# Pooled attention into a tanh-shrink MLP: batch 2's queries load behind batch 1's turns, batch 1's values go through GpSimd, the last queries load at a phase's end

## The chip, the cores and the metric

The kernel runs on one core of a Trainium2 chip. The metric is the device time of one execution in microseconds (us), the median of several runs. Engines are named as in the profile: PE is TensorE, PEld its weight loads, DVE is VectorE, ACT is ScalarE, POOL is GpSimd, and SP is SyncE, whose queue issues most of the DMAs.

## The reference

Eight batches, eight heads, 576 positions, head size 64. Keys and values are averaged over groups of 8 positions, which leaves 72 of them; attention runs over these, and its output goes through a two-layer network without biases, whose activation is h - tanh(h).

```python
k_p = k.reshape(B, H, Sp, pool, D).mean(axis=3)      # Sp = 576 / 8 = 72
v_p = v.reshape(B, H, Sp, pool, D).mean(axis=3)
scores = scale * np.matmul(q, k_p.transpose(0, 1, 3, 2))
scores = scores - np.max(scores, axis=-1, keepdims=True)
attn = np.exp(scores)
attn = attn / (np.sum(attn, axis=-1, keepdims=True) + 1e-09)
attn_out = np.matmul(attn, v_p)
x = attn_out.transpose(0, 2, 1, 3).reshape(B * S, H * D)   # 4608 x 512
h = x @ w_in                                               # 512 x 2048
out = (h - np.tanh(h)) @ w_out                             # 2048 x 512
```

## The kernel before

**Groups.** The 4608 rows are worked as nine groups of 512: group g below 8 is the first 512 positions of batch g, and group 8 collects the last 64 positions of all eight batches (the "tails", two batches to a tail block). A group has an h phase (16 blocks of four matmuls with `w1b`, `h_mms`, tanh on ACT and the subtraction on DVE in `h_act`) and an o phase (16 units of four matmuls with `w2b`, `o_mms`, whose banks are copied by `o_store` and stored from a list `stores`). While PE works on group g, the attention of batch g + 1 runs in between.

**Attention of a batch** is cut into four query blocks (five units where a tail block belongs to it: groups 1, 2, 4 and 6 carry tails 0, 1, 2 and 3). Each unit goes through the steps

- "s": scores on PE (`s_mms`), row maximum and subtraction on DVE (`s_shift`);
- "e": the exponential on ACT (`s_exp`) into the tile E;
- "t": the turn of E into ET by a DMA transpose that SP issues (`e_turn_dma`), for two units at once in the main loop;
- "a": weights times values on PE (`av_mms`, reads ET and VB), then reciprocal and multiply on DVE (`normalise`) into x_sb;
- "x": the turn of x_sb into xT, the h phase's operand, again a DMA transpose on SP (`x_turn_dma`).

**Order.** The schedule is written by hand: each engine runs its instructions in program order, and the framework only adds semaphores. In the main loop (line 697 on) a table `plan` says after which h block (negative keys, block i has key i - 16) or o unit (keys from 0) a step is issued. Group 0's o phase has a loop of its own (`for u in range(16)`, line 657), with batch 1's attention unit by unit: `s_unit` (each unit turned by itself) and `a_unit`. PSUM has eight banks; the scores of phase 0 use the pairs `PA = (0, 1)` and `PB = (2, 3)`, its output blocks banks 4 to 7.

**Loads.** `load_for(g)` issues on SP the values of batch g + 1, the queries and keys of batch g + 2, and for odd g the tail queries of that pair of batches. Values and keys are pooled by GpSimd (`pool_v`, `pool_k`) and placed in VB and, after a turn by DMA (`k_turn_dma`), in KB (`k_place_kT`). Queries are cast to bf16 by ACT (`q_cast`) and turned by DMA (`q_turn_dma`). Tail queries are loaded (`tail_pieces`), cast by GpSimd (`tail_cast`) and turned (`turn_tail`). For batch 1 some of this is done by PE: `q_turn_pe`, `k_turn_pe`, and `v_pool_pe`, which pools the values into a PSUM bank.

SP's order in group 0's o phase is thus: keys and queries of batch 2; the four turns of E; tail 0's queries; two x turns; the turns of batch 2's queries, of its keys and of tail 0; `load_for(1)`, with tail 1's queries last; four output stores; and then, in group 1, the first turn of batch 2.

## Time and profile before

| | |
|---|---|
| runs shown | 313.4, 314.0 and 1074.03 us; median 314.0 us |
| the profiled execution | 312.61 us, its span 310.9 us |
| granted TensorE clock, mean | 0.989 |
| busy: PE, DVE, ACT, POOL | 290.0, 181.0, 140.7, 109.4 us |
| group 1 starts its h phase | 61.09 us |
| group 2 | 95.34 us |

Times in the profile count from the span's start. In a row of the timeline the first number is the start, the second the time that the row covers, then come engine, line, operation, the tile written and the tile read, and in brackets how long the engine stood idle before it and what ended that. The list of waits gives who waited for whom, the total in us, how many times, and the longest. In the DMA rows the last number is the median time from issue to landing. Matmuls are pipelined, so the time from one start to the next is what a matmul costs PE.

### The profile page before, as it was taken

Reading aid. Unit: us, or ns where it says so; the run is one execution under the profiler, and the core shown is the slowest. Engines: PE = TensorE matmul, PEld = TensorE weight load, DVE = VectorE, ACT = ScalarE, POOL = GpSimd, SP = SyncE. Lnnn points to the kernel's source line nnn. Section 1 sums busy time; section 2 is a strip of 40 time slices with the busy share of each in tenths; the row PEclk is TensorE's granted clock in tenths of the full one; section 3 lists DMA queues with packets and bytes.
Section 4 is the critical chain, followed back from the end, with each engine's and each line's share of the span. In section 5 each row is a group of like instructions: output and inputs, shape, how many; then the busy total and the mean of one; then the engine's idle time right before and its main releaser. Section 6 shows DMA issues by size and latency. Waiting matters only on the chain.

```text
span 310.9 us, 4511 instructions
## 1 busy us (share of the span) xinstructions
PE 290.0 (93%) x1724; PEld 149.7 (48%) x1747; DVE 181.0 (58%) x251; ACT 140.7 (45%) x183; POOL 109.4 (35%) x97
## 2 busy tenths in 40 slices
PE   4779997999699998999999999999999999999995
PEld 1447954444354454445544554454445544444443
DVE  4596767469733993298419942984199427304700
ACT  1467744158323762267236632672364335315511
POOL 6545715019810592079108810791080000000000
PEclk9599999999999999999999999999999999999999
DMA  7999999989987978898999698978802640020023
GB/s 231 219 231 298 216 285 166 153 241 326 222 188 230 319 122 151 242 327 117 215 255 303 111 187 209 334 146 180 257 14 44 164 120 0 0 103 34 0 62 74
DMA packets 88981, 55.15 MB, mean 177 GB/s; under 512 B 62752, under 2 KB 76448, under 8 KB 88960
## 3 DMA queue, kind: packets, MB, share of 16 engines
q1 hardware_dynamic: 81648, 46.48, 61.2%
q0 software_dynamic: 6032, 7.60, 12.6%
q10 hardware_dynamic: 1280, 0.79, 0.8%
q8 instruction: 13, 0.21, 0.3%
q14 instruction: 8, 0.07, 0.1%
HBM read 36.70 MB, written 9.44 MB: 148 GB/s over the span
## 4 chain that ended last, share of the span: by engine, by line
PE 73%; DMA 14%; DVE 4%; ACT 3%; SPq 2%; issue 2%; ACTq 0%; DVEq 0%
PE PS L428 31%; PE PS L385 31%; DMA ET<-E 7%; DMA k_raw<-in_k_dram 5%; PE PS L338 4%; PE PS L274 2%; PE PS L407 2%; DMA xT<-x_sb 1%; PE PS L255 1%; DVE x_sb L360 1%; ACT E L302 1%; DMA ETl<-El 1%; DMA out_dram<-o_sb 1%; DVE sh L289 1%; DVE mx L286 1%
## 5 line engine op out<-in xcount | busy, mean ns | idle before, releaser
L428 PE MATMUL PS<-w2b,gT 128*128 128x512 bf16 (+2 forms) x570 | 131.7, 373 | 1.0
L399 DVE TENSOR_TENSOR gT<-PS,t_sb 128x1024 bf16<-128x1024 f32 x64 | 77.2, 1220 | 63.1 <-ACT t_sb L398 63.1
L385 PE MATMUL PS<-xT,w1b 128*128 128x512 bf16 x448 | 100.8, 379 | 0.3 <-DMA xT<-x_sb 0.2
L398 ACT ACTIVATE t_sb<-PS 128x1024 f32<-128x1024 f32 x64 | 65.6, 1025 | 43.3 <-PE PS L385 43.3
L428 PEld LDWEIGHTS <-gT 128*128 128x128 bf16 x592 | 54.3, 98 | 58.0 <-issue 0.8
L385 PEld LDWEIGHTS <-w1b 128*128 128x128 bf16 x512 | 49.3, 98 | 56.9 <-DMA xT<-x_sb 0.7
L449 ACT COPY o_sb<-PS 128x512 f32<-128x512 f32 x33 | 19.4, 587 | 83.9 <-PE PS L428 82.7
L207 POOL TENSOR_TENSOR v_raw<-v_raw 128x1280 f32<-128x1280 f32 x6 | 17.4, 2906 | 67.0 <-DMA v_raw<-in_v_dram 62.3
L302 ACT ACTIVATE E<-sh 128x576 bf16<-128x576 f32 x32 | 21.8, 683 | 21.4 <-DVE sh L289 21.4
L286 DVE TENSOR_REDUCE mx<-PS 128x8 f32<-128x576 f32 x36 | 27.0, 749 | 3.3 <-PE PS L274 3.3
L289 DVE TENSOR_TENSOR sh<-PS,mx 128x576 f32<-128x576 f32 x36 | 27.3, 758 | 1.2
L359 DVE RECIPROCAL rden<-PS 128x8 f32<-128x8 f32 x36 | 7.4, 206 | 32.4 <-PE PS L338 32.4
L192 POOL TENSOR_TENSOR k_raw<-k_raw 128x1280 f32<-128x1280 f32 x7 | 20.3, 2905 | 8.1 <-DMA k_raw<-in_k_dram 8.0
L360 DVE TENSOR_TENSOR x_sb<-PS,rden 128x512 bf16<-128x512 f32 x32 | 22.1, 691 | 1.1
L338 PE MATMUL PS<-VB,ET 128*128 128x130 bf16 (+2 forms) x192 | 16.7, 222 | 5.2 <-DMA ET<-E 4.8
L338 PEld LDWEIGHTS <-ET 128*128 128x128 bf16 x192 | 13.2, 98 | 13.0 <-DMA ET<-E 6.8
L243 ACT CAST q_bf<-q_raw 128x1024 bf16<-128x1024 f32 x14 | 14.5, 1040 | 5.9 <-DMA q_raw<-in_q_dram 5.9
L407 PE MATMUL PS<-xT,w1b 128*128 128x256 bf16 x128 | 15.3, 273 | 0.7 <-ACT xT L377 0.7
L229 POOL COPY KB<-kT 64x288 bf16<-64x288 bf16 x12 | 5.1, 424 | 26.3 <-DMA kT<-kd 26.0
L274 PEld LDWEIGHTS <-qT 128*128 128x128 bf16 x128 | 10.2, 100 | 7.9 <-ACT qT L520 0.8
L385 PE MATMUL PS<-xTt,w1b 128*128 128x512 bf16 x64 | 14.0, 379 | 0.0
L420 DVE TENSOR_TENSOR gT<-PS,t_sb 128x512 bf16<-128x512 f32 x16 | 10.9, 691 | 5.0 <-ACT t_sb L419 3.4
(72 smaller groups left out, 167.6 us busy)
## 6 DMA issues: line engine op xcount, KB each, us to landing
out_dram<-o_sb SPq DMA_DIRECT2D x32, 256.0 KB, 2.6
k_raw<-in_k_dram SPq DMA_DIRECT2D x14, 512.0 KB, 8.1
q_raw<-in_q_dram SPq DMA_DIRECT2D x13, 512.0 KB, 7.1
v_raw<-in_v_dram SPq DMA_DIRECT2D x12, 512.0 KB, 4.7
w1b<-in_moe_w_in_dram POOLq DMA_DIRECT2D x4, 512.0 KB, 8.9
w2b<-in_moe_w_out_dram POOLq DMA_DIRECT2D x4, 512.0 KB, 19.8
v_raw<-in_v_dram POOLq DMA_DIRECT2D x2, 512.0 KB, 13.8
k_raw<-in_k_dram POOLq DMA_DIRECT2D x1, 1024.0 KB, 13.4
```

Source lines behind the costliest of these rows:

```text
L192: eng.tensor_tensor(out=r[:, :, 0:4, :], in0=r[:, :, 0:4, :], in1=r[:, :, 4:8, :], op=ALU.add)
L286: nc.vector.reduce_max(out=mx.rearrange("p k h o -> p k (h o)"), in_=sc, axis=AX.X)
L289: nc.vector.tensor_tensor(out=sh[:, :, :, :], in0=sc, in1=mx.to_broadcast([128, 2, 4, G]), op=ALU.subtract)
L302: nc.scalar.activation(out=E[:, e, :, :].rearrange("p t c -> p (t c)")[:, 0:NK], in_=sh.rearrange("p k h c -> p (k h c)"), func=ACT.Exp, s ...
L338: nc.tensor.matmul(PS[ps, banks[half], D1 * h : D1 * (h + s1 - s0)], lhsT=ET[:, t, c0 : c0 + (ps.stop - ps.start)], rhs=VB[kb][:, t, s0:s1 ...
L360: nc.vector.tensor_tensor(out=x_sb, in0=ps[:, :, :, 0:D], in1=rden.to_broadcast([128, 2, 4, D]), op=ALU.mult,)
L385: nc.tensor.matmul(PS[:, bank, :].rearrange("p (j c) -> p j c", j=R), lhsT=w1b[:, fb, i * 128 : (i + 1) * 128], rhs=xT_of(g)[:, :, fb, :], ...
L398: nc.scalar.activation(out=t_sb[:, :, :], in_=ps, func=ACT.Tanh)
L399: nc.vector.tensor_sub(out=gT[:, i : i + 2, :], in0=ps, in1=t_sb[:, :, :])
L407: h_mm_last[0] = nc.tensor.matmul(PS[:, bank, 256 * s : 256 * s + 256].rearrange("p (j c) -> p j c", j=2), lhsT=w1b[:, fb, (2 * n + s) * 1 ...
L428: nc.tensor.matmul(PS[:, bank, 0 : c1 - c0], lhsT=gT[:, i, tb * 128 : (tb + 1) * 128], rhs=w2b[:, i, c0:c1], start=(i == 0), stop=(i == NH ...
L449: eng(out=o_sb[:, :], in_=PS[:, bank, :])
```

## The change

1. In the lead-in, the turned keys of batch 1 go to banks 6 and 7 instead of 0 and 1.
2. In group 0's o phase, batch 2's queries are no longer loaded ahead of it; SP issues them behind the fourth turn of E. Their cast, and the turns of batch 2's keys and queries (keys first now), are issued behind the second x turn.
3. Batch 1's values are pooled by PE right behind the first scores, in bank 7; ACT copies them to a new tile v_sm in SBUF, and GpSimd multiplies them into VB, where DVE did it from PSUM behind unit 3. GpSimd's pooling of batch 2's keys stands behind that.
4. The score units of phase 0 follow units 0, 1, 2 and 4 (before: 0, 1, 3 and 5), its values units 7, 8, 9 and 10 (before: 6, 7, 9 and 10).
5. Tail 0's queries are loaded behind the query turn and ahead of `load_for(1)`; their turn is issued behind it and ahead of the four stores.
6. Tails 1 to 3: `load_for` no longer loads them. They are loaded behind o unit 11 of groups 1, 3 and 5 and cast by GpSimd behind it (before: cast after o unit 0, turned at o unit 11), and turned in the h phase of the next group, behind the first turn of E.
7. The plan: the third values unit moves behind o unit 9, to the fourth. With a tail, the tail's exponential and turn move from o unit 5 to 4, and the third and fourth values units from 9 and 10 to 9. In group 1 the steps between the first exponential and the third scores are 2 to 3 h blocks later, the first two values units stand behind o units 6 and 7 (before: 4 and 5), and the last two behind 10.

```diff
+    v_sm = const.tile([128, NT, 1, D], FP32, name="v_sm")
...
-    kps = flat(0, NT * 128)
+    kps = flat(6, NT * 128)
     k_turn_pe(1, 0, NT, kps)
...
-            if g % 2:
-                r += tail_pieces((g + 2) // 2)
         run(r)
...
     after(load_rows(k_rows, k_raw[0], 2, 0, 2), held)
-    run(k_pieces(2)[1:] + q_pieces(2))
-    pool_k(2, nc.gpsimd)
+    run(k_pieces(2)[1:])
...
     def s_unit(n, bk):
         s_mms(s_block(1, n), bk)
         sh = s_shift(bk)
+        if n == 0:
+            nc.scalar.copy(
+                out=v_sm.rearrange("p t o d -> p (t o d)"),
+                in_=v_pool_pe(1, 7).rearrange("p t o d -> p (t o d)"),
+            )
+            v_place(1, v_sm, nc.gpsimd)
+            pool_k(2, nc.gpsimd)
         s_exp(sh, slot(4 + n))
         e_turn_dma(slot(4 + n), n % 2, n % 2 + 1)
...
-        if u == 3:
-            v_place(1, v_pool_pe(1, 0), nc.vector)
-            s_unit(2, PB)
-        if u == 5:
-            s_unit(3, PA)
+        if u == 2:
+            s_unit(2, PA)
+        if u == 4:
+            s_unit(3, PB)
+            run(q_pieces(2))
+        if u == 7:
+            a_unit(0, PA)
+        if u == 8:
+            a_unit(1, PB)
+            x_turn_dma(x1[0], 1, 0, 2)
+        if u == 9:
+            a_unit(2, PA)
+        if u == 10:
+            a_unit(3, PB)
+            x_turn_dma(x1[1], 1, 2, 2)
+            q_cast(2, se, 0, 2)
+            q_cast(2, se, 2, 4)
+            k_turn_dma(2)
+            k_place_kT(2, ge)
+            q_turn_dma(2)
             run(tail_pieces(0))
             tail_cast(0)
-        if u == 6:
-            a_unit(0, PB)
-            q_cast(2, se, 0, 2)
-            q_cast(2, se, 2, 4)
-        if u == 7:
-            a_unit(1, PA)
-            x_turn_dma(x1[0], 1, 0, 2)
-        if u == 9:
-            a_unit(2, PB)
-        if u == 10:
-            a_unit(3, PA)
-            x_turn_dma(x1[1], 1, 2, 2)
-            q_turn_dma(2)
-            k_turn_dma(2)
-            k_place_kT(2, ge)
-            turn_tail(0)
             load_for(1)
...
+    turn_tail(0)
     run(stores)
...
-                8: [("a", 2)],
-                9: [("a", 3), ("x", 1)],
+                9: [("a", 2), ("a", 3), ("x", 1)],
             }
             if g == 1:
-                plan[-10], plan[-7] = plan.pop(-12), plan.pop(-9) + plan.pop(-8)
+                plan[-10], plan[-7], plan[-5] = plan.pop(-12), plan.pop(-9), plan.pop(-8)
+                plan[-2], plan[-1] = [("e", 1), ("t", 0)], plan.pop(-3)
             if tail is not None:
                 units.append((s_tail(tail), av_tail(tail), slot_tl))
                 plan[3].append(("s", 4))
-                plan[5] += [("e", 4), ("t", 2)]
-                plan[10] = plan.pop(9)
-                plan[9] = plan.pop(8)
+                plan[4] += [("e", 4), ("t", 2)]
+                if g == 1:
+                    plan[6], plan[7] = plan[4][:1], plan.pop(5)
+                    plan[4] = plan[4][1:]
+                    plan[10] = plan.pop(9)
                 plan[12] = [("a", 4), ("x", 2)]
...
                 e_turn_dma(units[2 * n][2], 0, 2 if n < 2 else 1)
+                if tail and n == 0:
+                    turn_tail(tail)
...
                 pool_k(nb + 1, nc.gpsimd)
-                if nb % 2 == 0:
-                    tail_cast(nb // 2)
...
                 if u == 11 and nb % 2 == 0:
-                    turn_tail(nb // 2)
+                    run(tail_pieces(nb // 2))
+                    tail_cast(nb // 2)
```

## The prediction

> **What bounds the kernel now.** I read the page first, then what TensorE (PE) waits for, then its timeline, then the SP queue and the landing times of its DMAs. The page's first block, and two rows of PE's waits (us in all, times, longest):
>
> ```profile
> PE 290.0 (93%) x1724; PEld 149.7 (48%) x1747; DVE 181.0 (58%) x251; ACT 140.7 (45%) x183; POOL 109.4 (35%) x97
> ...
> PE PS L338 <- DMA ET<-E: 4.8, 4, 2.4
> ...
> PE PS L255 <- ACT qT L520: 0.7, 1, 0.7
> ```
>
> PE is busy for 93% of the span. Where the waits stand, in PE's timeline (start, us, matmuls; in brackets the idle time before them):
>
> ```profile
> 42.42 0.41 PE L274 MATMUL PS<-KB,qT 128*128 128x144 bf16 x4
> ...
> 45.51 1.25 PE L525 MATMUL PS<-v_raw,ident 128*128 128x320 bf16 x8
> ...
> 51.35 0.53 PE L338 MATMUL PS<-VB,ET 128*128 128x130 bf16 x6 [1.71 <-DMA ET<-E]
> ...
> 56.18 0.35 PEld L338 LDWEIGHTS <-ET 128*128 128x128 bf16 x6 [0.63 <-DMA ET<-E]
> ...
> 61.09 6.20 PE L385 MATMUL PS<-xT,w1b 128*128 128x512 bf16 x28
> ...
> 83.65 0.53 PE L338 MATMUL PS<-VB,ET 128*128 128x130 bf16 x6 [2.44 <-DMA ET<-E]
> ...
> 95.34 4.48 PE L385 MATMUL PS<-xT,w1b 128*128 128x512 bf16 x20
> ...
> 124.81 0.72 PE L338 MATMUL PS<-VB,ETl 128*64 128x130 bf16 x12 [1.36 <-DMA ETl<-El]
> ...
> 189.92 4.49 PE L385 MATMUL PS<-xT,w1b 128*128 128x512 bf16 x20 [0.24 <-DMA xT<-x_sb]
> ...
> 213.71 0.53 PE L338 MATMUL PS<-VB,ET 128*128 128x130 bf16 x6 [0.54 <-DMA ET<-E]
> ```
>
> and two rows of the chain of waits (start, us, instructions):
>
> ```profile
> 53.10 1.73 PE PS L428 x8
> ...
> 99.82 0.25 PE PS L274 x4
> ```
>
> All but the 0.7 us are waits for a DMA turn (transpose). The list names four for ET, 4.8 us in all; 1.71, 2.44 and 0.54 stand here, so the fourth is about 0.1. With 0.63 (the weight load of phase 0's fourth values unit), 1.36, 0.24 and 0.7 they add up to 7.7 us. No matmul is added or removed, and what else PE idles lies in the start and the last store, which the diff leaves alone: a gain can hardly exceed 7.7 us, 2.5%.
>
> **Phase 0 (output blocks of group 0, attention of batch 1; 41.4 to 61.09).** Its turns share the DMA engines with batch 2's query load, and SP issues everything in order:
>
> ```profile
> 45.64 7.18 SPq L311 DMA_TRANSPOSE ET<-E  x4
> 52.87 2.27 SPq L154 DMA_DIRECT2D tl_raw<-in_q_dram  x2
> ...
> 59.04 2.13 SPq L249 DMA_TRANSPOSE qT<-q_bf  x1
> ```
>
> The landing times of the DMAs issued between 34 and 64 (count, KB each, median us from issue):
>
> ```profile
> q_raw<-in_q_dram SPq DMA_DIRECT2D x2, 512.0 KB, 13.7
> tl_raw<-in_q_dram SPq DMA_DIRECT2D x2, 128.0 KB, 4.1
> ...
> ET<-E SPq DMA_TRANSPOSE x4, 4.7
> ...
> xT<-x_sb SPq DMA_TRANSPOSE x2, 3.3
> ...
> qT<-q_bf SPq DMA_TRANSPOSE x1, 4.5
> ```
>
> And ACT's casts of the queries:
>
> ```profile
> 51.50 1.98 ACT L243 CAST q_bf<-q_raw 128x1024 bf16<-128x1024 f32 x2
> ```
>
> The queries took 13.7 us, and ACT could cast them at 51.50; the first turn, issued at 45.64, ended in PE's row at 51.35, 5.7 us later. With the queries behind the fourth turn, I give the turns the median 4.7 us or less: the first lands by 50.3. In the new order PE reaches it after eight output blocks of four matmuls, four score units and the pooling of the values. By the chain's rows a block is 0.865 us (1.73 for eight matmuls) and a score unit 0.25; the pooling is 1.25. The first block stands ahead of the first score at 42.42, so it is there at 42.42 + 1.25 + 7 x 0.865 + 4 x 0.25 = 50.7. So 1.71 and 0.63 go, and the phase would end 2.3 us sooner, near 58.8. The keys' turn in other PSUM banks takes away the 0.7 us wait for ACT, but the score behind it still needs the copied keys, whose copies wait for the last subtraction on VectorE; I price that edit at nothing. Without that it would gain 0.7.
>
> The values of batch 1 get one ACT copy, which ends before ACT's first exponential could start, and a GpSimd multiply instead of VectorE's:
>
> ```profile
> 75.79 1.80 POOL L219 TENSOR_TENSOR VB<-v_raw,mask 128x960 bf16<-128x960 f32 x1
> 57.77 0.61 POOL L162 CAST tl_bf<-tl_raw 128x512 bf16<-128x512 f32 x1 [6.45 <-DMA tl_raw<-in_q_dram]
> ```
>
> 1.80 us from about 44.4 ends at 46.2, four before its reader. Batch 2's key pooling, behind it on GpSimd, comes about a microsecond later, and SP turns the keys only after the last x turn. Cost: nothing; if the values were later than 50.7, one for one.
>
> **What becomes late.** SP's four turns took 7.18 us from 45.64, to 52.8; with the pooling no longer between the second and third score, and one exponential after the other as before, I let them end at 52.2, and the queries go out then. Nearest rows for their landing: 6.0 us behind the values (below, batch 3's) and 13.7 above. I take 6.0, since by then no weights are left in flight: 58.2 (ends: 56 and 66). x's second turn goes out three blocks, four values units (0.53 at most) and about 1 us of normalising after 50.7, near 56, with 3.3 us to land, behind the queries, so I start the next h phase at 59.5 and not at 58.8. ACT's two casts (1.98) end at 60.3, SP's turn of the queries goes out then and lands 4.5 us later, as it did before, at 64.8. The first scores of the h phase stand behind seven h groups: 59.5 + 7 x 0.865 = 65.5. Hidden by 0.7 us. ACT's output copies queue behind the casts and are needed by the fifth h group at 63; hidden too.
>
> In a sentence that the sum does not need: the Trainium skill, DMA: Bandwidth & Descriptors, sections Specifications and Anatomy of one DMA, gives about 358 GB/s from HBM and 2 us fixed, so an estimate of 5 us for 1 MB, and the queries would land at 57.2; the sum would be the same within its bounds, as the wait below decides.
>
> **Group 1 (61.09 to 95.34).** SP's queue there:
>
> ```profile
> 62.88 1.22 SPq L165 DMA_TRANSPOSE tl_T<-tl_bf  x1
> 64.19 1.04 SPq L114 DMA_DIRECT2D v_raw<-in_v_dram  x2
> ...
> 68.83 1.69 SPq L154 DMA_DIRECT2D tl_raw<-in_q_dram  x2
> 70.62 4.09 SPq L452 DMA_DIRECT2D out_dram<-o_sb  x4
> 75.84 1.99 SPq L311 DMA_TRANSPOSE ET<-E  x1
> ...
> 83.31 1.36 SPq L311 DMA_TRANSPOSE ET<-E  x1
> ```
>
> and the landing times of what was issued between 64 and 76:
>
> ```profile
> q_raw<-in_q_dram SPq DMA_DIRECT2D x2, 512.0 KB, 6.0
> tl_raw<-in_q_dram SPq DMA_DIRECT2D x2, 128.0 KB, 8.4
> ...
> ET<-E SPq DMA_TRANSPOSE x1, 7.8
> ```
>
> The first turn of batch 2 is issued at 75.84 and lands 7.8 us later, at 83.6: it is drained behind the loads and four stores. In the new order the queries' turn (60.3 to 62.5) is followed by the tail queries (2.27 us of issue), so the value loads leave at 64.8, 0.6 later than before. Tail 1's two loads (1.69 us) no longer stand between the keys and the stores, tail 0's turn (1.22) does. The tail lands at 64.8 + 4.1 = 68.9 at the latest, GpSimd's cast adds 0.61, and SP comes to the turn at about 69.4, so hardly a wait. Net: +0.6 - 1.69 + 1.22, so the turn lands at 83.7; between 82 (only the lost tail counts) and 85.5 (the queries 2 us later). The scores of the second unit are now two h groups later, and their exponential stands behind a query cast, ready near 75.0, just ahead of 75.8.
>
> PE comes to the first values unit after output block 6 instead of 4, at 59.5 + 13.8 + 1.4 (five score units) + 6.05 = 80.8, and waits about 2.9 us to 83.7. So phase 0's gain is not additive: the wait swallows it. What counts is how much remains behind the landing: 95.34 - 83.65 = 11.69 us before, two output blocks fewer now, 9.96. Group 2 starts at 93.7: **-1.6 us**. The second pair's turn went out at 83.31 behind the first, and I leave it there: with 3.3 us like the x turns it lands near 87, ahead of its readers after block 10 (83.7 + 4 x 0.865 + two values units = 88). The x turn behind them goes out near 90 and lands by 93.5.
>
> **Groups 2 to 6.** The tail's exponential and turn go ahead of the output copy and of the first x turn, one block earlier, and ACT is free there: 1.36 goes. The third values unit moves one block (0.865) later, more than 0.1 and 0.54: both go. In the tail groups the last x turn is a block earlier, more than 0.24: goes. Together 1.36 + 0.1 + 0.54 + 0.24 = **-2.2 us**, or nothing of it if the tail's turn or a value comes as much later as it is moved. The tail's loads move ahead of the value loads (1.7 to 2.3 us of SP) in groups 1, 3 and 5, and its turn (1.22) ahead of a query turn; the values they delay have slack:
>
> ```profile
> 109.83 1.80 POOL L219 TENSOR_TENSOR VB<-v_raw,mask 128x960 bf16<-128x960 f32 x1
> ...
> 114.96 0.52 PE L338 MATMUL PS<-VB,ET 128*128 128x130 bf16 x6
> ```
>
> 111.6 to 114.96 is 3.3 us, the smallest cover of that edit; beyond it a late value costs one for one. The sum is -1.6 - 2.2 = -3.8 us. The profiled execution took 312.61 (span 310.9), so 308.8 on its scale; the median of the runs shown is 314.0, the lowest 313.4, their middle 313.7, and from there I predict 309.9.
>
> **Rivals.**
> *A. The queries come late.* A landing at 62 instead of 58.2 moves the value loads and all behind them by 3.8: group 2 starts at 97.5, +2.2, total 0.0: 313.7. For it: they took 13.7 once. Against: the w2b loads of that time are gone.
>
> *B. Slower: SP stands at tail 0's turn.* That turn now waits for a load, for GpSimd's cast, and has four stores and batch 2's first turn behind it in SP's order. It decides once the tail lands after about 76: then its turn (1.22), four stores and the E turn cannot go out before 80 and all of the gain is spent. With the 13.7 us that the queries once took, from 64: landing 77.7, cast 78.3, tail turn 79.5, half of the 4.09 that four stores took, so the E turn out at 81.6 and landed at 89.4. That is 5.7 later than forecast: -3.8 + 5.7 = +1.9, 315.6. Against it: 4.1 and 8.4 us are the tail's own rows.
>
> *C. The clock.* PE's longer wait at the first values unit may cost its clock. Start of the kernel and the old wait (window, length, busy time and count of each engine, granted clock, DMA share, GB/s):
>
> ```profile
> 8.00:10.00 2.00, 0.10 (x2) 0.11 (x3) 1.17 (x4) 0.83 (x1) 0.10 (x1) 0.50 1.20 252
> ...
> 12.00:14.00 2.00, 2.00 (x15) 1.10 (x13) 0.30 (x1) 1.47 (x3) 2.00 (x4) 0.50 1.24 205
> ...
> 82.00:84.00 2.00, 0.35 (x6) 0.35 (x7) 0.36 (x1) 0.00 (x0) 1.92 (x3) 1.00 1.11 250
> ```
>
> After idle gaps near the start the clock was 0.50 for the 4 us of work from 10 to 14; the 2.44 us wait left it at 1.00. If 2.9 us is past the edge, 4 us at half clock cost 2.0: 311.9. The Trainium skill, TensorE: Matmul & The Clock Gate, Part 1, puts the edge at an idle window of about 3.4 us and the recovery at as much busy time; by it 2.9 us is just safe, and this trace does not show the edge itself.
>
> *D. Everything goes.* If the first turn lands by 80.8, group 2 starts at 90.8, -4.5, with -2.2: 307.0. Against it: 1 MB of stores still stands ahead.
>
> **Numbers.** Forecast 0.55, A 0.17, B 0.07, C 0.12, D 0.09. A difference of 2%, about 6.3 us, is what a measurement tells from none: D alone (and luck in the forecast) is faster by that, 0.10; B must grow to twice its price, or A join it, to be slower by that, 0.05; within it 0.85. The range, 306.8 to 314.4, holds D's end, the forecast with turn landings of 82 to 85.5, C and most of A.
>
> **What would show it.** Right: no wait at the first and fourth values unit of phase 0, h of group 1 starting near 59.5, no wait for qT in it, the first values unit of group 1 at 83 to 84.5 after a wait of 2 to 3.5 us, group 2 at about 93.7, and no waits for ETl, ET or xT from there. Wrong: a PE wait for qT or xT near 60 to 66, SP idle ahead of tail 0's turn, a granted clock under 1 near 84, or GpSimd's values late in groups 2, 4 or 6.

## The result, and the profile after

| | before | changed |
|---|---|---|
| first chip: median (runs) | 314.16 us (313.4 to 314.32) | 310.0 us (309.31 to 310.66), ratio 0.9875 [0.9843, 0.9908] |
| second chip: median (runs) | 311.83 us (311.16 to 314.01) | 309.67 us (308.75 to 310.83), ratio 0.9927 [0.9901, 0.9953] |
| profiled execution (its span) | 312.61 (310.9) us | 310.13 (308.4) us, a second one 309.71 (308.0) us |

The comparison leaves out the run of 1074.03 us, which stands by itself; the median of 314.16 still counts it, without it it is 314.0. The changed kernel is faster by 0.5% to 1.6%, inside the 2% that the forecast called "no change", and its median is 0.1 us from the forecast. The profiled executions say less: 2.5 us between them, where 3.8 had been worked out.

The page's first block of the changed kernel, and a row of what PE waits for:

```profile
PE 292.1 (95%) x1747; PEld 150.4 (49%) x1747; DVE 179.5 (58%) x250; ACT 140.9 (46%) x184; POOL 111.2 (36%) x98
...
PE PS L339 <- DMA ET<-E: 2.7, 1, 2.7
```

Of the four waits for ET, 4.8 us, one is left, and it is longer than any before; the waits for ETl and for xT are no longer in the list. Two small ones have come, at the first score (the keys) and at the start of the h phase. PE's timeline, at the places shown of before (line numbers are one higher now):

```profile
42.59 0.41 PE L275 MATMUL PS<-KB,qT 128*128 128x144 bf16 x4 [0.88 <-ACT KB L230]
...
50.72 0.52 PE L339 MATMUL PS<-VB,ET 128*128 128x130 bf16 x6
...
54.44 0.53 PE L339 MATMUL PS<-VB,ET 128*128 128x130 bf16 x6
...
60.12 6.21 PE L386 MATMUL PS<-xT,w1b 128*128 128x512 bf16 x28 [0.84 <-DVE o_sb L450]
...
84.71 0.53 PE L339 MATMUL PS<-VB,ET 128*128 128x130 bf16 x6 [2.74 <-DMA ET<-E]
...
94.67 4.48 PE L386 MATMUL PS<-xT,w1b 128*128 128x512 bf16 x20
...
122.71 0.72 PE L339 MATMUL PS<-VB,ETl 128*64 128x130 bf16 x12
...
187.41 4.49 PE L386 MATMUL PS<-xT,w1b 128*128 128x512 bf16 x20
```

Phase 0's first values unit (50.72) and the fourth (54.44) start without a wait. The h phase of group 1 starts 0.97 us earlier than before, but its first values unit 1.06 us later. From that unit to the next group it is 94.67 - 84.71 = 9.96 us, where it was 11.69. Behind it no bracket stands any more, neither at the tail's values (122.71) nor at group 4's h phase (187.41).

When group 7 (its full operand, xT) and group 8 (the collected tails, xTt) start, from the rows of the h phase's line, first before, then changed (ns min/median/max, first and last start):

```profile
L385 PE MATMUL PS<-xT,w1b x4: 379/379/379, 251.8 to 252.4; 128*128 128x512 bf16 x4
...
L385 PE MATMUL PS<-xTt,w1b x3: 379/379/379, 279.4 to 279.8; 128*128 128x512 bf16 x3
```

```profile
L386 PE MATMUL PS<-xT,w1b x3: 378/380/380, 248.8 to 249.2; 128*128 128x512 bf16 x3
...
L386 PE MATMUL PS<-xTt,w1b x3: 378/379/380, 276.4 to 276.8; 128*128 128x512 bf16 x3
```

So the 2.5 us come about as follows. The first score stands 0.2 later (42.59 for 42.42). From there to group 2 it is 52.08 us instead of 52.92: -0.8. Groups 2 to 6, from group 2's start to group 7's, take 154.1 instead of 156.4: -2.3. Group 7 is the same, and from group 8's start to the end it is 32.0 instead of 31.5: +0.5. The second profiled execution of the changed kernel gives 51.92, 154.0 and 32.0. The last piece, which the diff doesn't touch, is 31.4 to 32.1 in all the executions profiled here, of whichever kernel. The -0.8 rests on one execution of the kernel before: with its group 0 and group 1 unchanged, the same stretch takes 52.33 us in experiment 4 and, less the 1.66 us of a fallen clock, 52.05 in experiment 3. So what phase 0 and group 1 gain is 0 to 1 us, within the scatter; only the -2.3 is clear of it.

What makes the first values unit of group 1 late stands in the SP queue:

```profile
45.80 6.01 SPq L312 DMA_TRANSPOSE ET<-E  x4
...
60.28 1.99 SPq L250 DMA_TRANSPOSE qT<-q_bf  x1
...
64.06 1.08 SPq L115 DMA_DIRECT2D v_raw<-in_v_dram  x2
...
71.82 3.03 SPq L453 DMA_DIRECT2D out_dram<-o_sb  x4
...
76.26 2.29 SPq L312 DMA_TRANSPOSE ET<-E  x1
```

and in the landing times of the DMAs issued from 34 to 60 and from 64 to 77 (the last two rows):

```profile
q_raw<-in_q_dram SPq DMA_DIRECT2D x2, 512.0 KB, 4.9
...
ET<-E SPq DMA_TRANSPOSE x4, 2.6
...
xT<-x_sb SPq DMA_TRANSPOSE x2, 4.6
...
tl_T<-tl_bf SPq DMA_TRANSPOSE x1, 9.2
...
ET<-E SPq DMA_TRANSPOSE x1, 8.4
```

Phase 0's turns land 2.6 us after issue with the query load out of their way, for 4.7 before; x's turns, with the load now ahead of them, take 4.6 for 3.3. The first turn of batch 2 went out at 76.26, landed 8.4 us later at 84.66, and PE goes on at 84.71. ACT's casts of the queries and the exponential that this turn waits for:

```profile
58.26 1.99 ACT L244 CAST q_bf<-q_raw 128x1024 bf16<-128x1024 f32 x2 [7.67 <-DMA q_raw<-in_q_dram]
...
75.56 0.68 ACT L303 ACTIVATE E<-sh 128x576 bf16<-128x576 f32 x1
```

### The profile page after: what moved, and what is told of

It reads as the page before. It is cut to its first block, busy times and chain, and to the rows that moved or that the text cites. A ratio compares the mean times of both kernels' runs of the same rounds, so it can differ in the third digit from the quotient of the medians.

```text
span 308.4 us, 4530 instructions
## 1 busy us (share of the span) xinstructions
PE 292.1 (95%) x1747; PEld 150.4 (49%) x1747; DVE 179.5 (58%) x250; ACT 140.9 (46%) x184; POOL 111.2 (36%) x98
## 4 chain that ended last, share of the span: by engine, by line
PE 83%; DMA 8%; DVE 3%; ACT 2%; SPq 2%; issue 1%; ACTq 0%; DVEq 0%
PE PS L429 38%; PE PS L386 31%; PE PS L339 4%; PE PS L408 3%; DMA ET<-E 3%; PE PS L275 3%; DMA q_raw<-in_q_dram 3%; DMA k_raw<-in_k_dram 2%; PE PS L256 1%; PE PS L526 1%; PE PS L468 1%; ACT E L303 1%; DVE gT L421 1%; DVE x_sb L361 1%; SPq L155 1%
## 5 line engine op out<-in xcount | busy, mean ns | idle before, releaser
L339 PE MATMUL PS<-VB,ET 128*128 128x130 bf16 (+2 forms) x192 | 15.7, 222 | 2.9 <-DMA ET<-E 2.7
L230 POOL COPY KB<-kT 64x288 bf16<-64x288 bf16 x12 | 5.1, 421 | 32.1 <-DMA kT<-kd 22.8
L275 PE MATMUL PS<-KB,qT 128*128 128x144 bf16 x128 | 13.4, 232 | 1.1 <-ACT KB L230 0.9
```

The costliest lines, as they stand in the source:

```text
L275: nc.tensor.matmul(PS[ps, banks[m // 2], KP * (m % 2) : KP * (m % 2) + KP], lhsT=qT[:, m, :], rhs=KB[kb][:, m, :], start=True, stop=True,)
L339: nc.tensor.matmul(PS[ps, banks[half], D1 * h : D1 * (h + s1 - s0)], lhsT=ET[:, t, c0 : c0 + (ps.stop - ps.start)], rhs=VB[kb][:, t, s0:s1 ...
```

## The experiments

The theory at the start: group 1's first values unit, which waits for a landing, sets group 2; what is put behind that unit decides there; the plan alone makes the gain in groups 2 to 6. The rivals: the clock, the tail's turn, and the query load as the cause of everything. Beside each kernel measured here, the kernel before ran on the same chip.

**1. The first two values units of group 1 back behind o units 4 and 5.**

```diff
-                    plan[6], plan[7] = plan[4][:1], plan.pop(5)
-                    plan[4] = plan[4][1:]
```

> The changed kernel, but in group 1 the first two values units stand behind output units 4 and 5 again, not 6 and 7. My theory (the landing of batch 2's first turn, 84.7 us in the changed kernel, sets group 1, and each output unit that stands behind it is paid after it): the turn lands at 84.7 as before, TensorE waits 2.74 + 1.73 = 4.5 us for it, and group 2 starts 1.7 us later, at 96.4, so 311.7 us. The first rival (what phase 0 saved carries through to the end, and the place of these units is of no account): 310.0 and group 2 at 94.7. The second rival (the clock falls in a wait of 4.5 us): some 4 us at half clock behind the wait, group 2 at 98, 313.7.

Measured: 312.91 us, ratio 1.0025 [0.9995, 1.0055], all of the gain gone. PE's timeline and the windows behind the wait (columns as in the prediction: granted clock third from the end):

```profile
83.88 0.53 PE L339 MATMUL PS<-VB,ET 128*128 128x130 bf16 x6 [4.20 <-DMA ET<-E]
...
97.22 2.97 PE L386 MATMUL PS<-xT,w1b 128*128 128x512 bf16 x13
```

```profile
84.00:86.00 2.00, 2.00 (x13) 1.03 (x12) 0.90 (x2) 0.06 (x1) 0.41 (x1) 0.62 1.25 273
86.00:88.00 2.00, 2.00 (x11) 0.95 (x9) 0.90 (x2) 0.53 (x1) 0.00 (x0) 0.53 0.80 157
```

The turn lands when it did (83.88, or 41.89 us after the first score, for 42.12 in the changed kernel): the units' place doesn't move it. But the wait is 4.20 us, the clock behind it 0.62 and 0.53, and from the unit to group 2 it is 13.34 us: 11.69 and 1.65 more. After the wait in the changed kernel the clock stayed whole:

```profile
84.00:86.00 2.00, 1.29 (x12) 0.82 (x13) 0.69 (x2) 0.00 (x0) 1.29 (x1) 1.00 1.09 242
```

**2. The same, with PE kept busy.** Sixteen matmuls on zeros in front of that unit, whose output nobody reads.

```diff
                 bk = PAIRS[a_pairs[n]]
+                if g == 1 and n == 0:
+                    fill(16, 7)
                 av_mms(sl, a, bk)
```

> The kernel with group 1's first values units behind output units 4 and 5 again (4.2 us of wait, granted clock 0.62 and 0.53 in the 4 us behind it), and 16 more matmuls on zeros (3.5 us at full clock, into a free bank) in that wait. If the clock fell because TensorE stood idle, it stays at 1.00, group 2 starts 53.4 to 53.8 us after phase 0's first score instead of 55.2, and the time is 1.5 us less, near 311.2 against 312.9. If the late part was something else (the turns behind, the DMA queues), the start of group 2 stays at 55.2 or later.

Measured: 311.28 us, ratio 0.9972 [0.9947, 0.9996]. The same rows as above:

```profile
79.88 3.62 PE L468 MATMUL PS<-zeros 128*128 128x512 bf16 x16
...
84.59 0.53 PE L339 MATMUL PS<-VB,ET 128*128 128x130 bf16 x6 [1.09 <-DMA ET<-E]
...
96.28 4.05 PE L386 MATMUL PS<-xT,w1b 128*128 128x512 bf16 x18
```

```profile
86.00:88.00 2.00, 2.00 (x15) 1.05 (x13) 0.99 (x3) 0.58 (x1) 0.00 (x0) 1.00 1.06 209
```

Now it is 96.28 - 84.59 = 11.69 us to group 2, exactly that of before, and the clock stays at 1.00. So the moved units are worth 11.69 - 9.96 = 1.73 us, two output blocks, as the prediction had it; and the 1.65 us on top in experiment 1 are the clock, which fell because PE stood idle. The medians of the two kernels differ by 1.6 us too (312.91 and 311.28, with 311.93 and 311.92 for the kernel before beside them). Counted from the first score, group 2 starts after 54.22 us and not after the 53.4 to 53.8 expected, since the turn landed 0.6 us later than in experiment 1, 42.53 us after that score instead of 41.89.

**3. The plan of groups 2 to 6 alone, put into the kernel before.**

```diff
-                8: [("a", 2)],
-                9: [("a", 3), ("x", 1)],
+                9: [("a", 2), ("a", 3), ("x", 1)],
             }
+            if g == 1:
+                plan[8], plan[9] = plan[9][:1], plan[9][1:]
...
-                plan[5] += [("e", 4), ("t", 2)]
-                plan[10] = plan.pop(9)
-                plan[9] = plan.pop(8)
+                if g == 1:
+                    plan[5] += [("e", 4), ("t", 2)]
+                    plan[10] = plan.pop(9)
+                    plan[9] = plan.pop(8)
+                else:
+                    plan[4] += [("e", 4), ("t", 2)]
```

> The kernel before, with only the plan of groups 2 to 6 changed: third values unit behind output unit 9, the tail's exponential and turn behind unit 4 instead of 5, third and fourth values units with a tail behind 9. Loads, tails, phase 0 and group 1 are as before. My theory: the waits of 1.36 (tail's turn, group 2), about 0.15 and 0.54 (second turn, groups 3 and 5) and 0.24 (x's turn ahead of group 5) go and group 2 still starts at 95.3: 2.2 us less than before, 311.9 against 314.1. Rival (these waits went because the tails' loads were moved, or because everything starts earlier): the waits stay in part, and less than 1 us is gained, over 313.

Measured: 311.23 us, ratio 0.9942 [0.991, 0.9974]. In its trace groups 2 to 6 take 153.97 us, 2.46 less than before, with no wait for a turn left in them: the plan does all of that part, and the tails' later loads and turns none of it. The profiled execution doesn't show it in its span, 310.3, because of group 1, which this kernel leaves as it was:

```profile
83.26 0.53 PE L338 MATMUL PS<-VB,ET 128*128 128x130 bf16 x6 [2.10 <-DMA ET<-E]
...
96.61 3.62 PE L385 MATMUL PS<-xT,w1b 128*128 128x512 bf16 x16
```

Here the clock fell behind a wait of only 2.10 us, and 13.35 us went to group 2, 1.66 more than in the profiled execution of before, whose wait was 2.44. Its ten runs lie in two groups, four at 308.9 to 309.6 and six at 311.2 to 312.0; the 19 runs of the kernel before beside them do too, 14 at 310.6 to 312.5 and five at 313.5 to 313.9. The medians of like groups differ by 2.4 us (309.33 and 311.78) and 2.3 us (311.47 and 313.74): in the runs, too, the plan is worth what its trace shows. And 309.33 is no more than the 309.67 and 310.0 of the changed kernel on other chips, so what the other edits add doesn't show in the times.

Why the clock fell here and not behind 2.44 us is seen when the windows are cut where the clock changes. In every trace these changes are whole multiples of 3.41 us apart (here at 16.00, 84.27 and 87.68), so the span can be read in pieces of that length; where no change is near, the pieces are counted on from the last one (in the changed kernel from 15.65). The piece with the wait and the one behind it in this experiment, then the piece with the most of the wait in the changed kernel (its clock stays at 1.00 behind it):

```profile
80.86:84.27 3.41, 1.31 (x11) 0.66 (x10) 1.82 (x4) 0.68 (x1) 3.25 (x4) 1.00 0.97 207
84.27:87.68 3.41, 3.41 (x14) 1.67 (x13) 1.39 (x3) 1.17 (x2) 0.98 (x3) 0.50 1.07 231
```

```profile
80.50:83.91 3.41, 1.47 (x7) 0.49 (x5) 2.21 (x4) 1.86 (x4) 3.25 (x3) 1.00 1.32 196
```

The clock fell behind pieces in which PE was busy for 1.31 us (here), 1.14 (experiment 6) and 0.60 (experiment 1). It stayed whole behind 1.47 and 1.59 us (the two executions of the changed kernel), 1.50 (experiment 7), 1.80 (experiment 5), and twice 2.20 in the kernel before, where a boundary cut the wait of 2.44 us in two. So it is not the length of the wait alone that decides but how much of it falls into one piece, and the pieces lie differently in each execution. The two groups of runs fit that; it isn't shown run by run.

**4. Nine such matmuls on zeros in the wait of the kernel before.** The edit is that of experiment 2, with `fill(9, 7)`.

> The kernel before, with nine more matmuls on zeros (1.9 us) ahead of the first values unit of group 1, in the wait of 2.4 us there. Its runs lie in two bands, 310.6 to 312.5 and 313.5 to 313.9. If the upper band is a fallen clock behind that wait, it goes: all runs at 310.6 to 312.5, median 0.3 to 0.5 us lower. If the wait is not what makes the bands, they stay, and nine matmuls too late for the turn's landing may cost up to 0.3 us.

```profile
80.17 2.10 PE L467 MATMUL PS<-zeros 128*128 128x512 bf16 x9
...
82.47 0.53 PE L338 MATMUL PS<-VB,ET 128*128 128x130 bf16 x6 [0.19 <-DMA ET<-E]
```

Measured: 311.31 us, ratio 0.9964 [0.9943, 0.9985]; all twelve runs lie between 310.65 and 311.92. Of the 26 runs of the kernel before beside it 8 lie above 312.9, up to 313.9. The upper group is gone when PE stays busy there. That these runs are the ones whose clock fell in group 1 is inferred: no execution of the kernel before with a fallen clock at that place was profiled. The mean granted clock of each run supports it: 0.983 or 0.984 in seven of the eight, 0.986 or more in the other 18 and in all twelve with the matmuls on zeros.

**5. The queries ahead of phase 0 again.** Everything else as changed.

```diff
-    run(k_pieces(2)[1:])
+    run(k_pieces(2)[1:] + q_pieces(2))
...
             s_unit(3, PB)
-            run(q_pieces(2))
```

> The changed kernel, but batch 2's queries are loaded ahead of phase 0's turns again, as in the kernel before; all else is as changed. My theory: moving them behind the turns gained little by itself, because the new order of units reaches the first turn only at 50.7. First turn lands near 51.4, a wait of 0.7 us; the casts need no wait, the queries' turn goes out near 57.5 instead of 60.3, the value loads near 61.3 instead of 64.1, x's second turn has no queries ahead of it and group 1 starts near 59.7. Batch 2's first turn cannot be issued before its exponential, near 75.7, but has 3 us less traffic ahead of it: landed near 82, group 2 at 92.2, 2.4 us sooner: 307.6. Rival (the move of the queries is what pays): phase 0's waits of 1.71 and 0.63 come back, group 2 at 96 to 97, 312 us.

Measured: 308.44 us, ratio 0.9881 [0.9838, 0.9925]: not slower than the changed kernel (0.9875 and 0.9927). PE's timeline, then the SP queue:

```profile
51.25 0.53 PE L339 MATMUL PS<-VB,ET 128*128 128x130 bf16 x6 [0.69 <-DMA ET<-E]
...
59.81 6.20 PE L386 MATMUL PS<-xT,w1b 128*128 128x512 bf16 x28
```

```profile
62.86 1.08 SPq L115 DMA_DIRECT2D v_raw<-in_v_dram  x2
```

A wait of 0.69 us is back in phase 0, but the one at the start of the h phase is gone, and the two nearly cancel. By the landing times, the query load costs whichever turn is in flight beside it: the E turns take 4.1 us here and 4.7 before, but 2.6 when the load is behind them; the x turns take 3.1 here and 4.6 with the load ahead of them. The value loads leave 1.2 us earlier, 0.9 counted from the first score; 2.8 was expected (61.3 for 64.1). The cast is no longer what they wait for, but SP still has x's, the keys' and the queries' turns to issue first. From the first score to group 2 it is 51.51 us, 0.4 to 0.6 less than changed; the turn landed near 83.8 and not near 82, so the 2.4 us that were expected did not come.

**6. Phase 0's part alone, with the plan and the tails of the later groups as before.** The diff's parts 6 and 7 are left out:

```diff
             r += q_pieces(g + 2) + k_pieces(g + 2)
+            if g % 2:
+                r += tail_pieces((g + 2) // 2)
...
             if g == 1:
-                plan[-10], plan[-7], plan[-5] = plan.pop(-12), plan.pop(-9), plan.pop(-8)
-                plan[-2], plan[-1] = [("e", 1), ("t", 0)], plan.pop(-3)
+                plan[-10], plan[-7] = plan.pop(-12), plan.pop(-9) + plan.pop(-8)
```

(and `plan` from 5 on, `tail_cast` and `turn_tail` as before).

> The changed kernel's phase 0 (keys' banks, queries behind the turns, values through GpSimd, order of the units, tail 0 late) with the plan of all later groups, and the loads, casts and turns of tails 1 to 3, as in the kernel before. My theory (group 1 is set by the landing of batch 2's first turn, not by the end of phase 0): group 1 starts 1.2 us sooner, but tail 1's loads stand ahead of the stores again and tail 0's turn too, so the first turn lands 1 us later than in the changed kernel, near 85.5, and with 11.7 us of work behind it group 2 starts near 97.2, 1.9 later than before; the wait is about 5 us, so the clock falls behind it for another 1.5 to 2 us. 314 to 316 us against 312. Rival (the time that phase 0 saves stays saved): 1.2 us faster than before, 310.7.

Measured: 316.29 us, ratio 1.0125 [1.008, 1.0169], slower than the kernel before. PE's timeline, the landing of tail 0's turn, and a window:

```profile
80.90 0.45 PE L275 MATMUL PS<-KB,tl_T 128*64 128x144 bf16 x8 [2.63 <-DMA tl_T<-tl_bf]
...
84.39 0.83 PE L339 MATMUL PS<-VB,ET 128*128 128x130 bf16 x6 [1.93 <-DMA ET<-E]
```

```profile
tl_T<-tl_bf SPq DMA_TRANSPOSE x1, 9.7
```

```profile
86.00:88.00 2.00, 2.00 (x11) 1.10 (x10) 0.54 (x3) 1.03 (x2) 0.00 (x0) 0.50 0.93 175
```

Group 1 starts as in the changed kernel, 1.1 us sooner than before. But tail 0's turn, now late in SP's order and behind tail 1's load, takes 9.7 us to land, and PE waits 2.63 us for it. That wait leaves PE busy for 1.14 us of a piece of 3.41, and the clock is at half from 82.04 to 88.87, two pieces. PE then waits 1.93 us for the first E turn, and with the values units at their old place 13.83 us follow, 11.69 and 2.14 for the clock: group 2 starts 3.4 us later than before, counted from the first score. The E turn itself landed 42.5 us after the first score, 0.4 later than in the changed kernel; 1 us was expected. It isn't the prediction's rival B: GpSimd had cast tail 0 by 67.5, and SP issued its turn at 71.13 right behind tail 1's load, so SP did not stand there for the tail.

**7. The tails as before, the rest as changed.**

```diff
             r += q_pieces(g + 2) + k_pieces(g + 2)
+            if g % 2:
+                r += tail_pieces((g + 2) // 2)
...
-                if tail and n == 0:
-                    turn_tail(tail)
...
+                if nb % 2 == 0:
+                    tail_cast(nb // 2)
...
-                    run(tail_pieces(nb // 2))
-                    tail_cast(nb // 2)
+                    turn_tail(nb // 2)
```

> The changed kernel, but tails 1 to 3 are loaded with the keys, cast behind output unit 0 and turned behind unit 11, as in the kernel before. My theory: groups 2 to 6 are as in the changed kernel, no waits there (the new plan took them away, not the tails); in group 1 tail 1's loads stand ahead of tail 0's turn and the stores again, the first turn lands about 1 us later, group 2 starts 53 to 53.5 us after phase 0's first score instead of 52.1, and with a wait of 3.7 us the clock may fall for 1.5 us more. 1 to 2.5 us slower than the changed kernel. Rival (the tails' place matters in every group): waits for tl_T, ET or VB in groups 3 and 5, 3 us or more.

Measured: 309.95 us, ratio 0.9942 [0.9916, 0.9969], beside the changed kernel's 0.9927 [0.9901, 0.9953]. From the first score to group 2 it is 52.48 us, 0.4 to 0.6 more (a wait of 1.07 for tail 0's turn, then 1.91 for ET); groups 2 to 6 take 154.13, the same. So the tails' move is worth half a microsecond in group 1, by this one trace; the medians don't tell it from nothing. The 1 us of later landing and the 1 to 2.5 us that were expected did not come.

**8. The four stores of group 0's last blocks behind batch 2's turns of E.** The output pool gets seven buffers instead of four.

```diff
     turn_tail(0)
-    run(stores)
...
+                if g == 1 and n == 2:
+                    run(stores)
```

> The changed kernel, but group 0's four output stores (1 MB) are issued behind batch 2's two turns and the tail's turn in group 1, not ahead of them; seven output buffers instead of four, so that nothing waits for the stores to land. My theory (the first turn lands when what was issued ahead of it has drained): 1 MB less ahead of it, some 3 us, so it lands near 81.5, the wait of 2.74 us goes and group 2 starts at 92.0: 307.3. The x turns then stand behind the stores and may land late for group 2 by up to 1 us. Rival (the turn itself takes that long, or waits on SP for the loads): it still lands at 84 or later and nothing is gained, 310.

```profile
81.53 0.52 PE L339 MATMUL PS<-VB,ET 128*128 128x130 bf16 x6
...
93.38 4.48 PE L386 MATMUL PS<-xT,w1b 128*128 128x512 bf16 x20 [1.73 <-DMA xT<-x_sb]
```

Measured: 308.6 us, ratio 0.9885 [0.9842, 0.9927]. The last wait is gone, the unit starts 39.5 us after the first score instead of 42.1. But 1.73 us come back at group 2's start: x's turn now has the stores ahead of it. So the stores ahead of the first turn made that wait, and it moves with them.

**9. The stores behind the x turns.** As 8, but the stores of group 0 are kept in a list of their own and issued behind group 1's second x turn.

```diff
-    run(stores)
+    late, stores[:] = list(stores), []
...
+                if g == 1 and n == 1:
+                    run(late)
```

> The changed kernel, but group 0's four output stores are issued behind the second x turn of batch 2 in group 1 (seven output buffers). My theory (in group 1 what counts is the bytes ahead of the turns in the DMA engines): with the stores behind the E turns alone, the wait of 2.74 us before the first values unit went, and 1.73 us came back as a wait for x's turn behind the stores; behind the x turns both go, and group 2 starts 49.5 us after phase 0's first score (before 52.9, changed 52.1), 2.6 us sooner than in the changed kernel. Ratio to before 0.981. The value loads of batch 3 come behind the stores, but have 3 us of cover. Rival (the x turn is late for itself, by SP's order): the wait for x stays above 1 us, ratio 0.988.

```profile
92.21 4.48 PE L386 MATMUL PS<-xT,w1b 128*128 128x512 bf16 x20
...
112.04 0.45 PE L275 MATMUL PS<-KB,tl_T 128*64 128x144 bf16 x8 [1.40 <-DMA tl_T<-tl_bf]
```

Measured: 309.12 us, ratio 0.9915 [0.9881, 0.9949]. Group 2 starts 50.2 us after the first score, 1.7 to 1.9 earlier than changed (49.5 was expected; a wait of 0.98 us for tail 0's turn stands in group 1), and most of that is given back. The loads issued at group 2's start stand behind the five stores in SP's order and go out at 95.75, where the changed kernel has 95.99; tail 1's turn behind them lands at 112.0, where it has 112.1. PE comes to it 2.4 us sooner and waits 1.40 us, and 0.32 us more for an x turn at the start of group 3.

**10. Experiments 5 and 9 together.**

> The changed kernel with batch 2's queries ahead of phase 0's turns again and group 0's stores behind batch 2's x turns (seven output buffers). My theory: what each gave alone (first values unit of group 1 0.6 us earlier; its wait gone, group 2 1.9 us earlier) adds in part: the value loads go out 0.9 us sooner, so tail 0's turn, for which the stores-behind version waited 0.98 us, is in time, and group 2 starts 49.3 to 49.8 us after the first score (changed 52.1). 0.5 us under the stores-behind version, ratio to before 0.987 to 0.990. Rival: the turns of phase 0 that land late behind the queries give it back, ratio 0.992.

```profile
91.43 4.48 PE L386 MATMUL PS<-xT,w1b 128*128 128x512 bf16 x20
```

Group 2 starts 49.4 us after the first score, the earliest of all, with the wait for tail 1's turn behind it still at 1.2. Measured: 308.24 us (307.47 to 308.87), ratio 0.9882 [0.9849, 0.9916], on the chip where the changed kernel gave 309.67 (308.75 to 310.83) and 0.9927. It is the lowest median measured; the two intervals overlap, so that it beats the changed kernel is likely and not certain.

**11. The values of batch 1 placed by DVE again**, straight from bank 7.

```diff
-            nc.scalar.copy(
-                out=v_sm.rearrange("p t o d -> p (t o d)"),
-                in_=v_pool_pe(1, 7).rearrange("p t o d -> p (t o d)"),
-            )
-            v_place(1, v_sm, nc.gpsimd)
+            v_place(1, v_pool_pe(1, 7), nc.vector)
```

> The changed kernel, but batch 1's values are placed by VectorE from PSUM again (at the new place, behind the first scores), without the ACT copy and GpSimd's multiply. My theory (that edit costs and gains nothing here): within 0.3 us of the changed kernel; the second unit's shift comes up to 1.2 us later on VectorE, and its turn has at most 1 us of cover, so a wait of up to 0.5 us may stand at the second values unit, which group 1's wait swallows. Rival (VectorE's 1.16 us decides): group 1 starts 1.2 us later, the first turn of batch 2 lands later by as much, +1.2 us.

**12. The changed kernel once more**, beside 7, 10 and 11 on one chip.

> The changed kernel once more, beside the kernels below. If the upper band of the kernel before (a clock that falls behind the wait of 2.4 us) is a part of what was measured as gain, the changed kernel with its wait of 2.7 us has two bands as well, near 308.5 and 310.5, and its ratio to before lies between 0.985 and 0.992. If its wait is safe, there is one band near 308.5.

Measured: 309.91 us for the DVE version, ratio 0.9915 [0.9881, 0.9948], and 309.67, 0.9927 [0.9901, 0.9953] for the changed kernel: no difference that can be told. Of the six runs of the changed kernel five lie at 308.75 to 309.71 and one at 310.83; the ratio is just above the 0.985 to 0.992 expected, and six runs don't tell one band from two. In the trace with DVE, VectorE's 1.15 us stand ahead of the second unit's maximum, the turns of E end later, and PE waits 0.83 us at the fourth values unit of phase 0 (at the second, up to 0.5, was expected); the wait for x's turn behind it is 0.22 us instead of 1.03, so group 1 starts within 0.2 us of where it does without the edit. What differs beyond that is a landing. The issue of batch 2's first turn and its landing, with DVE:

```profile
75.70 2.01 SPq L312 DMA_TRANSPOSE ET<-E  x1
```

```profile
ET<-E SPq DMA_TRANSPOSE x1, 7.5
```

and in the changed kernel:

```profile
75.66 2.26 SPq L312 DMA_TRANSPOSE ET<-E  x1
```

```profile
ET<-E SPq DMA_TRANSPOSE x1, 8.7
```

Issued at the same moment behind the same loads and stores, it landed 1.2 us sooner with DVE, and nothing in the record says why. The nine runs with DVE lie at 307.5 to 308.3 (three) and 309.5 to 311.1 (six). Whether the GpSimd edit helps at all is left open: its effect is smaller than this scatter.

## Why the prediction was right, and where it was not

**Phase 0.** Right in its mechanism: both waits went (the 0.63 us were idle time of the weight loads; PE itself lost only about 0.3 us there, from 55.02 + 0.865 to 56.18), the first values unit stood at 50.72 (50.7 predicted), the casts began at 58.26 (58.2), the query turn went out at 60.28 (60.3). The h phase began at 60.12 and not at 59.5: I had made x's second turn land behind the queries with the 3.3 us of before; issued at 56.0, it took 4.0. The profile puts the 0.84 us in front of the phase down to a copy on DVE; the list of waits of the second execution names the turn,

```profile
PE PS L386 <- DMA xT<-x_sb: 1.0, 1, 1.0
```

and with the queries ahead (experiment 5) the wait isn't there, though the same copy ends after the phase has begun. So it is the x turn. The keys' banks, priced at nothing, removed a wait of 0.7 and made one of 0.88.

**Group 1, the step that was mis-sized.** "The wait swallows it" held, and what is left behind the landing was 9.96 us to the digit. But of the -1.6 us at most -0.8 came (-1.0 in the second execution, and less beside experiments 3 and 4), because the landing was put at 83.7 and was 84.7. Two terms make up that microsecond. The exponential was ready at 76.24, behind the query cast, and not "near 75.0, just ahead of 75.8", so the turn went out at 76.26, 0.4 after that of before; the earlier value loads (64.06, not 64.8) did not matter. And it took 8.4 us to land, 8.7 in the second execution, where I carried over the 7.8 of one trace; with group 1 as before it is 6.3 and 7.1 us in experiments 3 and 4. Counted from the first score, PE gets the turn after 40.4 to 41.2 us in these two and the kernel before, and after 41.9 to 42.5 with the change (its two executions and experiments 1 and 2): the two blocks moved ahead of it give 1.73 us, and a landing about 1.4 us later takes most of that back. With 7.5 us to land in experiment 11 (after 40.8), this landing has a spread of over a microsecond, and the lower half of my bounds, 82 to 85.5, needed luck.

**Groups 2 to 6.** -2.2 predicted, -2.3 and -2.5 measured; every wait named went, by the plan alone (experiment 3). The GpSimd slack of 3.3 us was enough: no values came late.

**The sum and the scale.** -3.8 was predicted, and -2.5 is what the two profiled executions differ by: 0.8 us too much from group 1, 0.2 us lost ahead of the first score and 0.5 in the part that the diff doesn't touch. That 309.9 still met the median of 310.0 is because I started from 313.7, the middle of the runs shown, and those were high: the kernel before gives 311.83 to 311.93 where it is run 19 to 26 times, and 8 of 26 runs lie about 2 us higher. The prediction's own scale, 312.61 - 3.8 = 308.8, was 1.3 us too low. That the number met is luck: two errors of about the same size cancelled.

**The rivals.** A did not come: the queries took 4.9 us. The prediction's estimate of 5 us for them from the Trainium skill, DMA: Bandwidth & Descriptors, Anatomy of one DMA, agrees, though its 2 us stand there for DMAs that GpSimd issues, and these are SP's. B did not come in any run: GpSimd had always cast tail 0 before SP came to its turn (67.9 and 69.3 in the changed kernel). What that turn did cost is its own landing, 9.2 us in the changed kernel without a wait, and waits of 1.07 us in experiment 7 and 2.63 in experiment 6, where tail 1's load is ahead of it, and 0.98 in experiment 9. D's end is about what experiment 8 has for the first values unit (81.5), and other turns then became late. C did not come in the two profiled executions of the changed kernel, at waits of 2.74 and 2.38 us, and that is luck: 1.47 us of busy time in the piece with the wait, where 1.31 was too little in experiment 3. Whether other runs of it lost their clock isn't shown. The fall was seen in experiments 1, 3 and 6, and is inferred for some executions of the kernel before; its price, 1.65 us in 1 and 3, is near the 2.0 I gave, and near the 1.71 us that one piece of 3.41 at half clock loses. Part of the ratio on the first chip may be that the changed kernel loses its clock less often; that is not shown.

The Trainium skill, TensorE: Matmul & The Clock Gate, Part 1, puts the fall behind an idle window of some 3.4 us, free-running. The length of 3.41 us between the clock's changes agrees, and so does their place, which differs between executions. That the window must be idle doesn't: the clock fell behind pieces in which PE was busy for 1.31 and 1.14 us, within waits of 2.10 and 2.63 us. Here the measurement decides, and the prediction's "2.9 us is just safe" does not hold.

## What to carry to other kernels

Time won ahead of a wait for a transfer is not time won: count from the landing, and look how much work is left behind it; moving two blocks of work in front of the landing gave the full 1.73 us (experiment 2), while starting the group a microsecond sooner gave nothing. A landing taken from one trace is worth only its spread, over a microsecond here, which is as much as the whole of group 1's gain. A load or a store moved out of the way of one DMA turn is moved into the way of the next (E's, then x's, then the tail's), so follow the queue until a turn with slack is reached. And a PE wait of 2 us may have a second price, the clock, in some executions and not in others.

## What the runs showed of the hardware that was not expected

- The granted clock changed only at times whole multiples of 3.41 us apart, and it fell by the busy time of PE in such a piece: behind 0.60, 1.14 and 1.31 us, not behind 1.47 us or more. So a wait of 2.10 us cost the clock where it lay in one piece, and waits of 2.44 and 2.74 us that a boundary cut did not. A fall lasted one piece in experiments 1 and 3 and cost 1.65 us, and two pieces in experiment 6; with matmuls on zeros in the wait the clock stood at 1.00.
- A DMA turn on SP landed 2.6 us after issue with little beside it and 8.4 to 9.7 us behind loads and stores; the same turn at the same moment landed 7.5 or 8.7 us after issue in two executions. The issue itself held SP for 1.5 us a turn in a row of four, and for 1.2 to 2.4 us where one turn of E or of a tail stood alone in the changed kernel.
